# Output product of a second MoE layer: high and low weight halves in one 512-column operand, tokens in blocks of 128

## Chip, cores and metric

One core of a Trainium2 chip runs the whole program. The metric is the device time of one execution in microseconds, lower is better; three timed runs of the kernel before gave 1485.56, 1487.03 and 1487.63 us (median 1487.03).

## What is computed

An attention block between 512 tokens and 32 state rows for 8 batches and 8 heads, then two MoE layers without routing on its 4352 rows of 512 values:

```python
x = concat([xread, sread])                  # attention, 8 x (512 + 32) rows
h = np.maximum(x @ w_in, 0.0)               # 512 -> 2048
x = h * h @ w_out                           # 2048 -> 512
xn = x / rms * rms_g
g = xn @ w_gate                             # 512 -> 1536
silu = g * (1.0 / (1.0 + np.exp(-g)))
return silu * (xn @ w_val) @ w_out          # 1536 -> 512
```

## The kernel before

**Numbers as pairs.** Every operand of a product is split into a high and a low part in a reduced 32-bit float form (`split`, L121: a copy on ScalarE and a subtraction on VectorE). A product is three matmuls into the same bank of PSUM: high by high, high by low, low by high (`mm3`, L125).

**Stages.** Attention and the first MoE run batch by batch until about 735 us. Then come the gate and value products of the second MoE (`moe2_in`, L720): four groups s of two batches, each with 12 steps fc over the hidden width; both tokens of a pair and both weights are combined by a Strassen-like scheme of seven products (`PRODUCTS`, L567) in place of eight, with sums and differences of the operands made beforehand and seven products added into results by `recombine` (L591). In the last group the 256 state rows go along (`moe2_in_sb`, L739). `h_sums` (L762) makes seven operands of the hidden values of a pair of batches, and `h_store` (L775) puts them into DRAM (`hq_dr`).

**The output product before.** First the 256 state rows, with no Strassen scheme: `moe2_out_sb` (L884) makes 12 x 2 x 3 matmuls of 512 columns from tiles `hs`, which hold four steps each and are split by `split_hs` (L879). Then eight blocks blk of 256 tokens of two batches: `load_hb` (L829) reads for each of six weight parts m a tile `hb` (four operands) and a tile `hc` (three) in pieces of 256 floats, `split_hb` (L838) splits them, and `moe2_out` (L847) runs for m, then for the seven products k, then for two halves c of 128 tokens, three matmuls of 256 columns (L859). The token values are the stationary operand, so every matmul has a weight load of 128 columns before it. All seven products of a block accumulate over m in seven PSUM banks; on the last m `recombine` takes each into the tiles `ox` and `oy`, and the store of a batch's rows stands right behind its last addition (L877).

**Weights.** `w2_sums` (L792) makes the differences of the output weights during the first MoE, `w2_split` (L805) makes two high and two low tiles of each part m and stores them in DRAM, and `load_w2` (L813) brings the 24 tiles of 512 KB back for the output stage, where they stay.

**What sets the order.** The order is written out by hand: `put(position, step)` collects events, which are sorted by position and issued in that order on every engine's own queue. A unit of position is a step fc in the gate and value stage (n2 is its end), and one of the six parts m after it. Offsets stand in the table T. All DMAs go through one queue, that of SP, in this order, and each waits there for its data and for a free slot: all tiles come out of one pool of 54 slots of 4 KB per partition. PSUM has eight banks, taken in turn (`any_bank`, L576).

Of the kernel before, what the change touches and what calls it, by code (L numbers as in the profile page):

```python
# [16 lines left out]
P = 128  # L17
# [30 lines left out]
    wq0=-6.06, wq=-1.9, wq_gap=0.27,  # L48
    xl0=-7.97, xsum0=-6.06, xsp0=-3.95, xsp_gap0=0.62, xl=-8.77, xl_gap=0.03, xsum=-4.63, xsp=-3.3, xsp_gap=0.44,
    xsum_gap=0.18, tail=0.3, hsum=0.3, hst=1.47, sbl=-1.3, sbs=-1.03, hs=-1.05, hbl=-3.88, hbs0=-1.5, hbs1=-1.37,  # L50
    w2l=-6.87, w2l_gap=1.18, w2l_i=1.24,
# [6 lines left out]
def attention_moe_kernel(  # L58
# [31 lines left out]
    SB = B  # L90
# [606 lines left out]
    def split_xb(s, name):  # L697
        if (s, name) not in xb:
            return
        t = xb.pop((s, name))  # L700
        if s == SB:
            n = ntok[SB]
            hi = u([P, 2, 512], F32R, "hi")
            nc.scalar.copy(hi[:, :, :n], f(t)[:, :, :n])
            lo = u([P, 2, 512], F32R, "lo")
            nc.vector.tensor_tensor(lo[:, :, :n], f(t)[:, :, :n], f(hi)[:, :, :n], op=ALU.subtract)
        else:
            hi = hi_of(t)
            lo = lo_of(t, hi)
        xq[s, name] = (hi, lo)  # L710
# [28 lines left out]
    def moe2_in_sb(fc):  # L739
        cols = slice((fc % 2) * P, (fc % 2 + 1) * P)  # L740
# [14 lines left out]
        q, r = divmod(fc, 4)  # L755
        if r == 0:
            hs[q] = u([P, 4, 256], F32, "hs")
        t = u([P, 2, 512], F32, "rg")
        nc.scalar.activation(t[:, 0, :n], g, AF.Silu)
        nc.vector.tensor_tensor(hs[q][:, r, :], t[:, 0, :n], v, op=ALU.mult)  # L760
# [14 lines left out]
    def h_store(s, m):  # L775
# [9 lines left out]
        (m, i): dram.tile([P, 2, 512], F32, tag=f"w2_{m}_{i}", name=f"w2_dr{m}_{i}")  # L785
        for m in range(NF2 // 2)
        for i in range(4)
# [4 lines left out]
    def w2_sums(m):  # L792
# [10 lines left out]
        w2s[m] = (w, t.rearrange("p (a q) m -> p a (q m)", a=2))  # L803

    def w2_split(m, i):  # L805
        after(("w2s", m, i))
        t = w2s[m][i]
        hi = hi_of(t)
        lo = lo_of(t, hi)
        nc.sync.dma_start(w2_dr[m, 2 * i], f(hi))  # L810
        nc.sync.dma_start(w2_dr[m, 2 * i + 1], f(lo))

    def load_w2(m, i):  # L813
        after(("ldw2", m, i), ("w2s", m, i // 2))
        w2q[m, i] = u([P, 2, 512], F32R, "w2")
        nc.sync.dma_start(f(w2q[m, i]), w2_dr[m, i])  # L816

    B_AT = dict(b11=(0, 0), b21=(0, 2), b22=(0, 3), t1=(2, 0), t2=(2, 1), t3=(2, 2), t4=(2, 3))

    def w2_part(m, name):  # L820
        i, q = B_AT[name]
        return tuple(
            w2q[m, i + j].rearrange("p a (q m) -> p (a q) m", q=2)[:, q, :] for j in range(2)
        )


    hb = {}

    def load_hb(blk, m):  # L829
        s, ob = divmod(blk, 2)  # L830
        cols = slice(256 * ob, 256 * ob + 256)
        after(("ldhb", blk, m), ("hst", s, m))
        t = [u([P, 4, 256], F32, "hb"), u([P, 4, 256], F32, "hc")]
        nc.sync.dma_start(t[0], hq_dr[s, m][:, :4, cols])
        nc.sync.dma_start(t[1][:, :3, :], hq_dr[s, m][:, 4:, cols])
        hb[blk, m] = t

    def split_hb(blk, m, i):  # L838
        t = hb[blk, m][i]
        n = 4 - i  # L840
        hi, lo = u([P, 4, 256], F32R, "hh"), u([P, 4, 256], F32R, "hl")
        split(t[:, :n, :], hi[:, :n, :], lo[:, :n, :])
        hb[blk, m][i] = (hi, lo)

    acc2 = {}

    def moe2_out(blk, m, k):  # L847
        a, b = PRODUCTS[k]
        last = m == NF2 // 2 - 1
        if m == 0:  # L850
            acc2[blk, k] = any_bank("o2")
        ps = acc2[blk, k]
        i, q = divmod(A_ROW.index(a), 4)
        hi, lo = (t[:, q, :] for t in hb[blk, m][i])
        w_hi, w_lo = w2_part(m, b)
        for c in range(2):
            o = ps[:, 256 * c : 256 * c + 256]
            cols = slice(c * P, (c + 1) * P)
            mm = lambda l, r, start, stop: nc.tensor.matmul(  # L859
                o, l, r, start=start, stop=stop, skip_group_check=True  # L860
            )
            mm(hi[:, cols], w_hi, m == 0 and c == 0, False)
            mm(hi[:, cols], w_lo, False, False)
            mm(lo[:, cols], w_hi, False, last)
        if not last:
            return
# [3 lines left out]
        pv = ps.rearrange("p (c d) -> p c d", c=2)  # L870
        recombine(k, pv, (ox[:, :, :256], ox[:, :, 256:]), (oy[:, :, :256], oy[:, :, 256:]))
        s, ob = divmod(blk, 2)
        for i, done in ((0, 5), (1, 6)):
            if k == done:
                b = 2 * s + i
                rows = out[b * NT : b * NT + S, :].rearrange("(p c) m -> p c m", c=4)
                nc.sync.dma_start(rows[:, 2 * ob : 2 * ob + 2, :], acc2[blk][i])  # L877

    def split_hs(q):  # L879
        hi, lo = u([P, 4, 256], F32R, "hh"), u([P, 4, 256], F32R, "hl")  # L880
        split(hs[q], hi, lo)
        hs[q] = (hi, lo)

    def moe2_out_sb(fc):  # L884
        if fc == 0:
            acc2[SB, 0], acc2[SB, 1] = any_bank("o2"), any_bank("o2")
        q, r = divmod(fc, 4)
        hi, lo = hs[q]
        w_hi, w_lo = w2q[fc // 2, 0][:, fc % 2, :], w2q[fc // 2, 1][:, fc % 2, :]
        for c in range(2):  # L890
            cols = slice(c * P, (c + 1) * P)
            mm3(acc2[SB, c], hi[:, r, cols], lo[:, r, cols], w_hi, w_lo, fc == 0, fc == NF2 - 1)
# [290 lines left out]
```

## Time and profile before

| | us |
|---|---|
| median of three runs | 1487.03 |
| lowest, highest | 1485.56, 1487.63 |
| the profiled execution, its own time | 1484.66 |
| its span, first to last instruction | 1482.6 |

The profile is one execution. The span leaves out 2.1 us at its edges; the profiled execution lies 0.9 us under the lowest timed run. A row of a group by line gives the engine, the operation, output <- inputs with their shapes and count, then the busy time, the mean duration of one and the idle time before it. The duration of a matmul is modelled and longer than the distance between two starts; the distance is read in a timeline. PE is TensorE, PEld its weight loads, DVE is VectorE, ACT is ScalarE, SPq is the DMA queue.

### The profile page before, as it was taken

The numbers are of one execution on the slowest core, as the hardware profiler recorded it, in microseconds if no ns is written. First come the engines' busy times: TensorE is split into PE (matmuls) and PEld (weight loads), VectorE is DVE, ScalarE is ACT, GpSimd is POOL, SyncE is SP. The second block draws the span as 40 slices with busy tenths as digits, with TensorE's granted clock in tenths as the row PEclk, the third lists the DMA queues.
The fourth block names the chain that finished last, engine by engine and source line by source line (L and its number), as shares of the span: only waits on it lengthen the run. The fifth ranks groups of instructions, "written<-read, shape, count | busy, mean of one in ns | idle before, by whom it ended". The sixth has DMA issues, their size and how long they took to land. (4 is left out here: it accounts for less than half of the span.)

```text
span 1482.6 us, 20652 instructions
## 1 busy us (share of the span) xinstructions
PE 1447.2 (98%) x7706; PEld 1248.6 (84%) x7706; DVE 1125.2 (76%) x1654; ACT 783.0 (53%) x1186; POOL 0.7 (0%) x6
## 2 busy tenths in 40 slices
PE   4899999999999999999999999999999999999998
PEld 2688888888888888889987888888888888999998
DVE  7997878999998999874778878978965664565554
ACT  5988768888888888874522211312311123434331
POOL 0000000000000000000000000000000000000000
PEclk7999999999999999999999999999999999999999
DMA  8886443464555555452957897797786869567753
GB/s 321 291 282 226 149 163 121 163 235 166 226 176 219 178 220 180 170 208 72 355 213 279 324 347 282 284 354 279 264 315 221 292 238 339 182 218 242 241 188 107
DMA packets 138420, 345.82 MB, mean 233 GB/s; under 512 B 12112, under 2 KB 56144, under 8 KB 138320
## 3 DMA queue, kind: packets, MB, share of 16 engines
q1 hardware_dynamic: 138320, 344.51, 64.6%
q8 instruction: 60, 0.98, 0.3%
q14 instruction: 40, 0.33, 0.1%
HBM read 229.12 MB, written 115.34 MB: 232 GB/s over the span
## 5 line engine op out<-in xcount | busy, mean ns | idle before, releaser
L126 PE MATMUL p<-hi,wq 128*128 128x512 f32 x672 | 261.7, 389 | 2.0 <-DVE hx L594 2.0
L127 PE MATMUL p<-lo,wq 128*128 128x512 f32 x672 | 261.6, 389 | 0.0
L128 PE MATMUL p<-hi,wq 128*128 128x512 f32 x672 | 261.4, 389 | 0.0
L859 PE MATMUL o<-w,hh 128*128 128x256 f32 x1344 | 242.1, 283 | 0.8 <-ACT hh L122 0.8
L734 ACT ACTIVATE hx<-hx 128x1024 f32<-128x1024 f32 x48 | 50.9, 1061 | 332.9 <-DVE hx L594 332.9
L126 PE MATMUL o<-hl,wh 128*128 128x512 f32 (+1 forms) x576 | 218.8, 380 | 1.1 <-DVE x L518 0.8
L128 PE MATMUL o<-hl,wl 128*128 128x512 f32 (+1 forms) x576 | 217.6, 378 | 0.0
L127 PE MATMUL o<-hl,wh 128*128 128x512 f32 (+1 forms) x576 | 217.5, 378 | 0.0
L859 PEld LDWEIGHTS o<-w,hh 128*128 128x128 f32 x1344 | 209.6, 192 | 1.3 <-ACT hh L122 1.3
L859 PE MATMUL o<-w,hl 128*128 128x256 f32 x672 | 190.4, 283 | 0.8 <-DVE hl L123 0.8
L594 DVE TENSOR_TENSOR hx<-hx,p 128x512 f32<-128x512 f32 x192 | 128.9, 683 | 52.6 <-PE p L128 49.6
L126 PEld LDWEIGHTS p<-hi,wq 128*128 128x128 f32 x672 | 126.2, 188 | 28.2 <-DVE hx L594 2.4
L128 PEld LDWEIGHTS p<-hi,wq 128*128 128x128 f32 x672 | 126.2, 188 | 26.4
L127 PEld LDWEIGHTS p<-lo,wq 128*128 128x128 f32 x672 | 126.2, 188 | 25.5
L490 DVE TENSOR_TENSOR hl<-rg,hl 128x512 fp32r<-128x512 f32 (+1 forms) x144 | 94.6, 657 | 54.3 <-ACT hl L489 53.4
L859 PEld LDWEIGHTS o<-w,hl 128*128 128x128 f32 x672 | 129.0, 192 | 1.1 <-DVE hl L123 1.0
L126 PEld LDWEIGHTS o<-hl,wh 128*128 128x128 f32 x576 | 108.4, 188 | 22.8 <-DVE x L518 2.8
L128 PEld LDWEIGHTS o<-hl,wl 128*128 128x128 f32 x576 | 108.4, 188 | 20.3
L127 PEld LDWEIGHTS o<-hl,wh 128*128 128x128 f32 x576 | 108.4, 188 | 19.8
L126 PE MATMUL h<-at,ph 128*128 128x512 f32 x256 | 102.1, 399 | 5.0 <-ACT pst L260 5.0
L123 DVE TENSOR_TENSOR hl<-hb,hh 128x1024 fp32r<-128x1024 f32 x48 | 58.7, 1222 | 57.1 <-ACT hh L122 57.1
L122 ACT CAST hh<-hb 128x1024 fp32r<-128x1024 f32 x48 | 50.4, 1050 | 95.9 <-DMA hb<-hq_dr 94.6
(169 smaller groups left out, 2592.9 us busy)
## 6 DMA issues: line engine op xcount, KB each, us to landing
wq<-wq_dr SPq DMA_DIRECT2D x168, 512.0 KB, 7.2
hq_dr<-hy SPq DMA_DIRECT2D x48, 512.0 KB, 3.6
hb<-hq_dr SPq DMA_DIRECT2D x48, 512.0 KB, 8.5
hc<-hq_dr SPq DMA_DIRECT2D x48, 384.0 KB, 8.7
raw<-in_moe_w_out_dram SPq DMA_DIRECT2D x30, 512.0 KB, 6.6
p_dr<-pst SPq DMA_DIRECT2D x56, 256.0 KB, 5.5
praw<-p_dr SPq DMA_DIRECT2D x28, 512.0 KB, 5.3
wq_dr<-hi SPq DMA_DIRECT2D x24, 512.0 KB, 2.9
```

What stands on the lines that cost most here:

```text
L122: nc.scalar.copy(hi, src)
L123: nc.vector.tensor_tensor(lo, src, f(hi), op=ALU.subtract)
L126: nc.tensor.matmul(ps, lh, rh, start=start, stop=False)
L127: nc.tensor.matmul(ps, lh, rl, start=False, stop=False)
L128: nc.tensor.matmul(ps, ll, rh, start=False, stop=stop)
L490: nc.vector.tensor_tensor(t[:, 1, :n], rg[:, 1, :n], f(t[:, 0, :n]), op=ALU.subtract)
L594: add = lambda o, i, p: nc.vector.tensor_tensor(o, i, p, op=ALU.add)
L734: nc.scalar.activation(x, x, AF.Silu)
L859: mm = lambda l, r, start, stop: nc.tensor.matmul(o, l, r, start=start, stop=stop, skip_group_check=True)
```

## The change

The output product takes 128 tokens at a time: 16 blocks of tokens, and before them one block with the state rows, which now goes through the seven products too (`hs_sums` makes its four further operands on the chip). The weights' high and low halves lie side by side, so one matmul of 512 columns multiplies the tokens' high part by both, and a second one of 256 columns multiplies the low part by the high half; `recombine` works on 512 columns with both halves, and one more addition folds the two halves before the store. A block runs in two halves of three parts m, with k outside m. Loads of the token tiles are one DMA of 448 KB with pieces of 128 floats for a block and part, placed earlier by a lead that grows over the first blocks; splits likewise; stores are placed 1.5 units behind. Weight tiles: 21 in place of 24. Offsets in the gate and value stage change as well. Below, unchanged lines and blank ones are thinned out, and the removal of `split_hs` and `moe2_out_sb`, which stood where the dots are, is left out.

```diff
@@ -45,10 +45,11 @@
-    wq0=-6.06, wq=-1.9, wq_gap=0.27,
-    xl0=-7.97, xsum0=-6.06, xsp0=-3.95, xsp_gap0=0.62, xl=-8.77, xl_gap=0.03, xsum=-4.63, xsp=-3.3, xsp_gap=0.44,
-    xsum_gap=0.18, tail=0.3, hsum=0.3, hst=1.47, sbl=-1.3, sbs=-1.03, hs=-1.05, hbl=-3.88, hbs0=-1.5, hbs1=-1.37,
-    w2l=-6.87, w2l_gap=1.18, w2l_i=1.24,
+    wq0=-6.06, wq=-3, wq_gap=0.33,
+    xl0=-7.97, xsum0=-6.09, xsp0=-3.95, xsp_gap0=0.62, xl=-8.78, xl_gap=0.03, xsum=-6.57, xsp=-4.14, xsp_gap=0.62,
+    xsum_gap=0.11, tail=0.3, hsum=0.43, hst=1.88, sbl=-2.06, sbs=-0.91, hss=0.2,
+    hbl=-8, hbl_gap=1.0, hbl_e=1.0, hbs=-4.8, hbs_gap=1.0, hbs_e=0.4, w2a=-4, ost=1.5, w2b=-1.6, 
+    w2l_gap=.6, w2l_i=.12,
 )
@@ -752,12 +752,23 @@
         product(g, "a12", "b21", False)
         product(v, "s1", "b11", True)
         product(v, "a22", "t4", False)
-        q, r = divmod(fc, 4)
+        m, r = divmod(fc, 2)
         if r == 0:
-            hs[q] = u([P, 4, 256], F32, "hs")
+            hs[m] = u([P, 7, P], F32, "hs")
         t = u([P, 2, 512], F32, "rg")
         nc.scalar.activation(t[:, 0, :n], g, AF.Silu)
-        nc.vector.tensor_tensor(hs[q][:, r, :], t[:, 0, :n], v, op=ALU.mult)
+        both = hs[m][:, 2 * r : 2 * r + 2, :]
+        halves = lambda ap: ap.rearrange("p (c t) -> p c t", c=2)
+        nc.vector.tensor_tensor(both, halves(t[:, 0, :n]), halves(v), op=ALU.mult)
+    def hs_sums(m):
+        after(("hs", m), ("sb", 2 * m), ("sb", 2 * m + 1))
+        a = [hs[m][:, i, :] for i in range(7)]
+        sub = lambda o, i, j: nc.vector.tensor_tensor(a[o], a[i], a[j], op=ALU.subtract)
+        nc.vector.tensor_tensor(a[4], a[1], a[3], op=ALU.add)
+        sub(5, 4, 0)
+        sub(1, 0, 1)
+        sub(6, 2, 5)
     def h_sums(s, m):
@@ -782,9 +793,9 @@
     w2_dr = {
-        (m, i): dram.tile([P, 2, 512], F32, tag=f"w2_{m}_{i}", name=f"w2_dr{m}_{i}")
+        (m, i): dram.tile([P, 2, 2, 256], F32, tag=f"w2_{m}_{i}", name=f"w2_dr{m}_{i}")
         for m in range(NF2 // 2)
-        for i in range(4)
+        for i in range(3 + (m + 1) % 2)
     }
     w2s = {}
     w2q = {}
@@ -800,105 +811,96 @@
         sub(t[:, 2, :], b22, b12)
         sub(t[:, 1, :], b22, t[:, 0, :])
         sub(t[:, 3, :], b21, t[:, 1, :])
-        w2s[m] = (w, t.rearrange("p (a q) m -> p a (q m)", a=2))
+        w2s[m] = (b[:, :, :256], t[:, :2, :], t[:, 2:, :], b[:, 1:, 256:])
     def w2_split(m, i):
         after(("w2s", m, i))
-        t = w2s[m][i]
-        hi = hi_of(t)
-        lo = lo_of(t, hi)
-        nc.sync.dma_start(w2_dr[m, 2 * i], f(hi))
-        nc.sync.dma_start(w2_dr[m, 2 * i + 1], f(lo))
+        src = w2s[m][i]
+        n = src.shape[1]
+        t = u([P, 2, 2, 256], F32R, "w2s")
+        split(src, t[:, :n, 0, :], t[:, :n, 1, :])
+        if i == 3:
+            nc.sync.dma_start(w2_dr[m - m % 2, 3][:, m % 2], f(t)[:, 0])
+            return
+        nc.sync.dma_start(w2_dr[m, i], f(t))
     def load_w2(m, i):
-        after(("ldw2", m, i), ("w2s", m, i // 2))
-        w2q[m, i] = u([P, 2, 512], F32R, "w2")
+        if i == 3 and m % 2:
+            return
+        after(("ldw2", m, i), ("w2s", m, i), ("w2s", m + (i == 3), i))
+        w2q[m, i] = u([P, 2, 2, 256], F32R, "w2")
         nc.sync.dma_start(f(w2q[m, i]), w2_dr[m, i])
-    B_AT = dict(b11=(0, 0), b21=(0, 2), b22=(0, 3), t1=(2, 0), t2=(2, 1), t3=(2, 2), t4=(2, 3))
+    B_AT = dict(b11=(0, 0), b21=(0, 1), t1=(1, 0), t2=(1, 1), t3=(2, 0), t4=(2, 1), b22=(3, 0))
     def w2_part(m, name):
         i, q = B_AT[name]
-        return tuple(
-            w2q[m, i + j].rearrange("p a (q m) -> p (a q) m", q=2)[:, q, :] for j in range(2)
-        )
+        if i == 3:
+            m, q = m - m % 2, m % 2
+        return w2q[m, i].rearrange("p q j d -> p q (j d)")[:, q, :]
     hb = {}
+    hq = {}
     def load_hb(blk, m):
-        s, ob = divmod(blk, 2)
-        cols = slice(256 * ob, 256 * ob + 256)
+        s, c = divmod(blk, 4)
         after(("ldhb", blk, m), ("hst", s, m))
-        t = [u([P, 4, 256], F32, "hb"), u([P, 4, 256], F32, "hc")]
-        nc.sync.dma_start(t[0], hq_dr[s, m][:, :4, cols])
-        nc.sync.dma_start(t[1][:, :3, :], hq_dr[s, m][:, 4:, cols])
-        hb[blk, m] = t
-    def split_hb(blk, m, i):
-        t = hb[blk, m][i]
-        n = 4 - i
-        hi, lo = u([P, 4, 256], F32R, "hh"), u([P, 4, 256], F32R, "hl")
-        split(t[:, :n, :], hi[:, :n, :], lo[:, :n, :])
-        hb[blk, m][i] = (hi, lo)
+        hb[blk, m] = u([P, 7, P], F32, "hb")
+        nc.sync.dma_start(hb[blk, m], hq_dr[s, m][:, :, c * P : (c + 1) * P])
+    def split_hb(blk, m):
+        hi, lo = u([P, 7, P], F32R, "hh"), u([P, 7, P], F32R, "hl")
+        if blk == 2 * B:
+            after(("hsplit", m), ("hs", m))
+            split(hs.pop(m), hi, lo)
+        else:
+            split(hb.pop((blk, m)), hi, lo)
+        hq[blk, m] = (hi, lo)
     acc2 = {}
-    def moe2_out(blk, m, k):
+    HALF = NF2 // 4
+    def moe2_out(blk, half, k):
         a, b = PRODUCTS[k]
-        last = m == NF2 // 2 - 1
-        if m == 0:
+        if half == 0:
             acc2[blk, k] = any_bank("o2")
         ps = acc2[blk, k]
-        i, q = divmod(A_ROW.index(a), 4)
-        hi, lo = (t[:, q, :] for t in hb[blk, m][i])
-        w_hi, w_lo = w2_part(m, b)
-        for c in range(2):
-            o = ps[:, 256 * c : 256 * c + 256]
-            cols = slice(c * P, (c + 1) * P)
-            mm = lambda l, r, start, stop: nc.tensor.matmul(
+        i = A_ROW.index(a)
+        for m in range(half * HALF, (half + 1) * HALF):
+            hi, lo = hq[blk, m]
+            w = w2_part(m, b)
+            mm = lambda o, l, r, start, stop: nc.tensor.matmul(
                 o, l, r, start=start, stop=stop, skip_group_check=True
             )
-            mm(hi[:, cols], w_hi, m == 0 and c == 0, False)
-            mm(hi[:, cols], w_lo, False, False)
-            mm(lo[:, cols], w_hi, False, last)
-        if not last:
+            mm(ps, hi[:, i, :], w, m == 0, False)
+            mm(ps[:, :256], lo[:, i, :], w[:, :256], False, m == 2 * HALF - 1)
+        if half == 0:
             return
         if k == 0:
             acc2[blk] = [u([P, 2, 512], F32, "ox"), u([P, 2, 512], F32, "oy")]
         ox, oy = acc2[blk]
-        pv = ps.rearrange("p (c d) -> p c d", c=2)
-        recombine(k, pv, (ox[:, :, :256], ox[:, :, 256:]), (oy[:, :, :256], oy[:, :, 256:]))
-        s, ob = divmod(blk, 2)
+        recombine(k, ps, (ox[:, 0, :], ox[:, 1, :]), (oy[:, 0, :], oy[:, 1, :]))
         for i, done in ((0, 5), (1, 6)):
             if k == done:
-                b = 2 * s + i
-                rows = out[b * NT : b * NT + S, :].rearrange("(p c) m -> p c m", c=4)
-                nc.sync.dma_start(rows[:, 2 * ob : 2 * ob + 2, :], acc2[blk][i])
...
+                t = acc2[blk][i]
+                o = t[:, :, :256]
+                nc.vector.tensor_tensor(o, o, t[:, :, 256:], op=ALU.add)
+    def store_out(blk, i):
+        o = acc2[blk][i][:, :, :256]
+        halves = lambda rows: rows.rearrange("p (a d) -> p a d", a=2)
+        if blk == 2 * B:
+            for q in range(4):
+                r0 = (4 * i + q) * NT + S
+                nc.sync.dma_start(halves(out[r0 : r0 + NS, :]), o[32 * q : 32 * q + 32])
             return
+        s, c = divmod(blk, 4)
+        r0 = (2 * s + i) * NT
+        rows = out[r0 : r0 + S, :].rearrange("(p c) m -> p c m", c=4)
+        nc.sync.dma_start(halves(rows[:, c, :]), o)
     sources = {"win": w_in, "wout": w_out, "wg": w_gate, "wv": w_val, "w2": w_out2}
@@ -1000,21 +1002,25 @@
     for name in ("b11", "b21", "t4"):
         put(e + T["sbs"] + 0.3, split_xb, SB, name)
     nout = NF2 // 2
-    for fc in range(NF2):
-        put(n2 + fc / 2, moe2_out_sb, fc)
-    for q in range(NF2 // 4):
-        put(n2 + 2 * q + T["hs"], split_hs, q)
-    for blk in range(B):
-        e = n2 + (blk + 1) * nout
+    for m in range(nout):
+        put(n2 - NF2 + 2 * m + 2 + T["hss"], hs_sums, m)
+    for q, blk in enumerate([2 * B] + list(range(2 * B))):
+        e = n2 + q * nout
+        early = min(max(q - 1, 0), 3)
         for m in range(nout):
+            h, r = divmod(m, HALF)
+            if blk < 2 * B:
+                put(e + HALF * h + T["hbl"] - T["hbl_e"] * early + T["hbl_gap"] * r, load_hb, blk, m)
+            put(e + HALF * h + T["hbs"] - T["hbs_e"] * early + T["hbs_gap"] * r, split_hb, blk, m)
+        for h in range(2):
             for k in range(7):
-                put(e + m + k / 7, moe2_out, blk, m, k)
-            put(e + m + T["hbl"], load_hb, blk, m)
-            put(e + m + T["hbs0"], split_hb, blk, m, 0)
-            put(e + m + T["hbs1"], split_hb, blk, m, 1)
+                put(e + HALF * (h + k / 7), moe2_out, blk, h, k)
+        for i in range(2):
+            put(e + HALF * (1 + (5 + i) / 7) + (T["ost"] if q < 2 * B else 0.0), store_out, blk, i)
     for m in range(nout):
         for i in range(4):
-            put(n2 + T["w2l"] + T["w2l_gap"] * m + T["w2l_i"] * i, load_w2, m, i)
+            h, r = divmod(m, HALF)
+            put(n2 + T["w2b" if h else "w2a"] + T["w2l_gap"] * r + T["w2l_i"] * i, load_w2, m, i)
     halves = ("xt", "st", "toka", "tokb", "at", "ex", "r2", "e2t", "xn", "sr")
@@ -1059,7 +1065,7 @@
             put(pos + T["dsp"] + T["dsp_gap"] * m, wq_split, c2, m)
         convert(pos + T["e0"], ("w2", c2), split=False)
         put(pos + T["e_sum"], w2_sums, c2)
-        for i in range(2):
+        for i in range(4):
             put(pos + T["e_sp"] + T["e_spgap"] * i, w2_split, c2, i)
     for fq in range(NFQ1):
         for k2 in range(2):
```

## Rows read from the trace of the kernel before

**Rows 1.** Page, busy us of each engine over the span
```profile
PE 1447.2 (98%) x7706; PEld 1248.6 (84%) x7706; DVE 1125.2 (76%) x1654; ACT 783.0 (53%) x1186; POOL 0.7 (0%) x6
```

**Rows 2.** Chain of waits that ended last, pieces: start us, us, what
```profile
1224.56 7.99 DMA hb<-hq_dr
...
1234.99 241.38 PE o L859 x2008
```

**Rows 3.** Groups by line, second output product: xcount | busy us, mean ns
```profile
L859 PE MATMUL o<-w,hh 128*128 128x256 f32 x1344 | 242.1, 283 | 0.8 <-ACT hh L122 0.8
L859 PE MATMUL o<-w,hl 128*128 128x256 f32 x672 | 190.4, 283 | 0.8 <-DVE hl L123 0.8
L126 PE MATMUL o<-w,hh 128*128 128x512 f32 x24 | 9.3, 390 | 0.0
```

**Rows 4.** Timeline of TensorE, 512 columns: start us, us, what
```profile
999.83 0.39 PE L128 MATMUL p<-hi,wq 128*128 128x512 f32 x1
...
1003.91 0.39 PE L128 MATMUL p<-hi,wq 128*128 128x512 f32 x1
```

**Rows 5.** Busy us of each engine by stretch, clock, DMA
```profile
core 0: us, PE busy (x) PEld busy (x) DVE busy (x) ACT busy (x) POOL busy (x), PEclk, DMA share, GB/s
965.00:1080.00 115.00, 115.00 (x520) 95.74 (x519) 96.67 (x134) 26.50 (x34) 0.00 (x0) 1.00 0.81 303
1080.00:1216.00 136.00, 136.00 (x723) 117.79 (x722) 83.99 (x123) 25.00 (x37) 0.00 (x0) 1.00 0.70 253
1216.00:1235.00 19.00, 17.41 (x80) 14.03 (x78) 6.47 (x9) 3.79 (x5) 0.00 (x0) 1.00 1.04 397
1265.00:1295.00 30.00, 30.00 (x253) 30.00 (x252) 16.51 (x20) 11.04 (x14) 0.00 (x0) 1.00 0.69 220
```

**Rows 6.** Timeline of TensorE where the token output product starts
```profile
1232.51 0.39 PE L128 MATMUL o<-w,hl 128*128 128x512 f32 x1
1233.73 0.51 PE L859 MATMUL o<-w,hh 128*128 128x256 f32 x2 [0.84 <-ACT hh L122]
1234.99 0.39 PE L859 MATMUL o<-w,hl 128*128 128x256 f32 x1 [0.76 <-DVE hl L123]
```

**Rows 7.** Timeline of the DMA queue SP: start us, us, issues
```profile
1224.56 0.46 SPq L834 DMA_DIRECT2D hb<-hq_dr  x1
...
1254.43 1.27 SPq L835 DMA_DIRECT2D hc<-hq_dr  x1
1268.00 0.36 SPq L877 DMA_DIRECT2D out_dram<-ox  x1
```

**Rows 8.** Waits of SP: us in total, times, longest us
```profile
SPq L877 <- DVE ox L594: 123.0, 8, 23.7
...
SPq L816 <- PE p L128: 23.7, 4, 13.8
```

**Rows 9.** Timeline of TensorE at a stop in the gate product
```profile
805.11 0.39 PE L128 MATMUL p<-hi,wq 128*128 128x512 f32 x1
807.49 0.47 PE L126 MATMUL p<-hi,wq 128*128 128x512 f32 x1 [1.99 <-DVE hx L594]
```

**Rows 10.** Groups by line, VectorE and ScalarE: xcount | busy us, mean ns
```profile
L123 DVE TENSOR_TENSOR hl<-hb,hh 128x1024 fp32r<-128x1024 f32 x48 | 58.7, 1222 | 57.1 <-ACT hh L122 57.1
L123 DVE TENSOR_TENSOR hl<-hc,hh 128x768 fp32r<-128x768 f32 x48 | 45.7, 952 | 1.4 <-ACT hh L122 1.4
L122 ACT CAST hh<-hb 128x1024 fp32r<-128x1024 f32 x48 | 50.4, 1050 | 95.9 <-DMA hb<-hq_dr 94.6 <-DMA hc<-hq_dr 0.7 <-PE o L859 0.7
L594 DVE TENSOR_TENSOR ox<-ox,o 128x512 f32<-128x512 f32 x32 | 21.8, 684 | 61.7 <-PE o L859 60.8
```

**Rows 11.** DMA issues: KB each, median us to landing
```profile
hb<-hq_dr SPq DMA_DIRECT2D x48, 512.0 KB, 8.5
...
out_dram<-oy SPq DMA_DIRECT2D x8, 512.0 KB, 4.0
```

**Rows 12.** Timeline of the end
```profile
1478.27 0.35 SPq L877 DMA_DIRECT2D out_dram<-oy  x1
```

More of the change, by code (lines that the diff above doesn't have):

```diff
@@ L701, in split_xb @@
         if s == SB:
[L702 to L706, printed above, removed]
+            both = u([P, 2, 2, ntok[SB]], F32R, "hl")
+            hi, lo = both[:, 0], both[:, 1]
+            split(f(t)[:, :, : ntok[SB]], hi, lo)
         else:
@@ L739, in moe2_in_sb @@
     def moe2_in_sb(fc):
+        after(("sb", fc))
         cols = slice((fc % 2) * P, (fc % 2 + 1) * P)
@@ L869, in moe2_out @@
         ox, oy = acc2[blk]
-        pv = ps.rearrange("p (c d) -> p c d", c=2)
-        recombine(k, pv, (ox[:, :, :256], ox[:, :, 256:]), (oy[:, :, :256], oy[:, :, 256:]))
-        s, ob = divmod(blk, 2)
+        recombine(k, ps, (ox[:, 0, :], ox[:, 1, :]), (oy[:, 0, :], oy[:, 1, :]))
         for i, done in ((0, 5), (1, 6)):
             if k == done:
-                b = 2 * s + i
-                rows = out[b * NT : b * NT + S, :].rearrange("(p c) m -> p c m", c=4)
-                nc.sync.dma_start(rows[:, 2 * ob : 2 * ob + 2, :], acc2[blk][i])
[L879 to L892, printed above, removed]
-        if fc < NF2 - 1:
-            return
-        t = u([P, 2, 512], F32, "os")
-        nc.scalar.copy(t[:, 0, :], acc2[SB, 0])
-        nc.vector.tensor_copy(t[:, 1, :], acc2[SB, 1])
-        for c in range(2):
-            for q in range(4):
-                r0 = (4 * c + q) * NT + S
-                nc.sync.dma_start(out[r0 : r0 + NS, :], t[32 * q : 32 * q + 32, c, :])
+                t = acc2[blk][i]
[8 more added lines that the diff above has]
+                nc.sync.dma_start(halves(out[r0 : r0 + NS, :]), o[32 * q : 32 * q + 32])
+            return
+        s, c = divmod(blk, 4)
+        r0 = (2 * s + i) * NT
+        rows = out[r0 : r0 + S, :].rearrange("(p c) m -> p c m", c=4)
+        nc.sync.dma_start(halves(rows[:, c, :]), o)
     sources = {"win": w_in, "wout": w_out, "wg": w_gate, "wv": w_val, "w2": w_out2}
```

## Prediction

> **What bounds the kernel now.** I read the page first: TensorE is busy for 98% of the span [rows 1], and in the stages that the change touches the granted clock is 1.00, so it runs at its upper level of 2.4 GHz [rows 5]. At 98% only two things can shorten the kernel: less work on TensorE, or fewer of its stops. The chain of waits says the same of the stage that is changed: it ends in one unbroken piece of 2008 matmuls of line 859 in 241.38 us, that is 120.2 ns each [rows 2], and before it stands a load of a token tile. The groups by line give the counts: 1344 and 672 matmuls of 256 columns, and 24 (three times, once for each line of `mm3`) of 512 columns for the state rows [rows 3]. Their mean durations (283 and 390 ns) are modelled and overlap; what counts is the distance of starts.
>
> **The price of a matmul.** In the 512-column timeline 18 distances take 1003.91 - 999.83 = 4.08 us, so 226.7 ns each [rows 4]. With 256 columns it is 120.2 ns [rows 2]. The difference is 106.5 ns for 256 columns, which is 2.4 columns per ns; so each matmul costs its columns plus a fixed 13.7 ns, with a new weight load before each in both cases. The change keeps the number of columns and takes away a third of the matmuls, so the fixed part is what it can win.
>
> The Trainium skill, TensorE: Matmul & The Clock Gate, in the section "Wait — 56ns, not 53.3ns?", gives a fixed part of about 2.5 ns for warm back-to-back matmuls. This case's rows show 13.7 ns at both sizes; by the page, as an estimate, 672 matmuls less would give 1.7 us and the state rows 1.9 us, 3.6 us where terms 1 and 2 below have 10.9.
>
> **Term 1, token blocks: -9.2 us.** Before, 128 tokens, one product and one part m cost 3 x 120.2 = 360.6 ns. After, one matmul of 512 and one of 256 columns: 226.7 + 120.2 = 346.9 ns. There are 16 x 6 x 7 = 672 such groups: 672 x 13.7 = 9.2 us. Lower and upper end are close, since both prices are measured at full clock; the one open point is whether the weights of a 512-column matmul load in the shadow of a 256-column one, and in the present stage every load does just that, with a new one each 120 ns.
>
> **Term 2, state rows: -1.7 us.** Before 72 matmuls of 512 columns [rows 3, 4]: 16.3 us. After, seven products: 42 pairs x 346.9 = 14.6 us. The price for it, additions on VectorE and larger splits, lies beside TensorE in a stage where VectorE has room (last group, below).
>
> **Term 3, the start of the output product: -0.6 us.** Now TensorE stops twice here, 0.84 + 0.76 us by the waits [rows 6], because the first token tile is issued at 1224.56 and lands 8 us later [rows 2, 7]; it stands behind weight loads that waited 23.7 us in all for slots that TensorE frees [rows 8]. After, the first token tiles are put in front of the second half of the weight loads and have 14.6 us of state rows as cover, so the 1.6 us should go. What is late next are the weights: the state rows used to need 12 of the tiles over 16 us, now they need 11 in their first 7.3 us and the other 10 by then. If the ten (5.2 MB) came only after n2, at the 350 GB/s that 512 KB loads reach in a burst, they would take 15 us and stop TensorE for 7.7 us. They are placed 1.6 units, some 20 us, ahead of n2, and that is nearest to the present small stop; I leave 1 us of new stop. Ends: -1.6 and +6.
>
> **Term 4, offsets in the gate and value product: -1.0 us.** TensorE has one stop there, 1.99 us, behind VectorE [rows 9]; the sums of the next group's operands pile up with the fold work. They move 1.9 units, about 18 us, earlier, and the weight loads 1.1 units. VectorE is 84% busy in this stage [rows 5], so the pile may shrink or arise elsewhere. Ends: -2.0 and +1.5; I take half the gain.
>
> **Term 5, the end: -0.3 us.** The last store is issued at 1478.27 [rows 12] and a store of 512 KB lands after 4.0 us [rows 11]. After, the fold of both halves adds one more addition of 512 columns, 0.68 us [rows 10], and the last stores are 256 KB each, some 0.7 to 1.5 us less to move for the two. Ends: -1 and +0.5.
>
> **What costs nothing, and its cover.** VectorE, for a block of 14.57 us (42 x 346.9 ns): six splits of 896 elements, between 952 ns for 768 and 1222 ns for 1024 [rows 10], so 1087 ns each, 6.5 us; seven folds and two additions of 0.684 us, 6.2 us; 12.7 us, 87%, against 55% now (16.51 of 30 us [rows 5]). The folds, which wait for TensorE, come in the second half of a block only, so VectorE falls behind there by some 3 us and makes it up in the first half of the next; a bank is needed again about three units, 7 us, after its fold was due. If VectorE fell more than that behind, TensorE would wait for banks. ScalarE has six copies of about 0.94 us (1.05 us for 1024 elements [rows 10]) and one more: no bound. The DMA queue: as many token loads as now (96), with 448 KB each. The stores now stand on SP right behind the fold they wait for, 123.0 us of waiting in eight pieces [rows 8], and the next block's loads queue behind: 1254.43 to 1268.00 nothing is issued [rows 7], and then twelve come in a burst. TensorE doesn't wait for that even now, so moving stores by 1.5 units gives nothing by itself, but it spreads the loads, which the next point needs. The four splits of a weight part in place of two handle fewer elements (1792 for 2048) and lie in the first MoE beside TensorE.
>
> **Pieces of 512 bytes.** Token loads now come in pieces of 1 KB: share 0.69 at 220 GB/s is 51 ns for a piece on one of 16 DMA engines; in the stage with pieces of mostly 4 KB, share 0.81 at 303 GB/s is 175 ns [rows 5]. The line through both is 10 ns plus 41 ns per KB, so 31 ns for 512 bytes. No row has a 512-byte piece: it lies between half of 51 and 51. By 31 ns a block's 5376 pieces take 10.4 us on 16 engines, its stores 1.6: 12 of 14.57 us, hidden. By 51 ns they take 17.3 + 1.6 = 18.9 us and the loads set the pace. I take 31, on the line between the two rows; up to 38 ns the loads stay within a block's time and cost nothing.
>
> **Sum.** -9.2 - 1.7 - 0.6 - 1.0 - 0.3 = -12.8 us. The profiled execution took 1484.66 us (its span is 1482.6), so 1471.9 there. The timed runs have their median 2.4 us above it, at 1487.03; I put the same difference on top: **1474.2 us**.
>
> **Rivals.**
> 1. **Weights late for the state rows.** The stop of term 3 at its full size: -9.2 - 1.7 + 6 - 1.0 - 0.3 = -6.2 us gives 1480.8. For it: the weight loads wait for slots today, and the stretch around 1216 to 1235 has a full DMA share (1.04 [rows 5]). Against: three fewer weight tiles are moved, and their place in the queue is 20 us ahead. Chance 0.11.
> 2. **Slower: the 512-byte pieces cost as much as 1 KB.** A block takes 18.9 instead of 14.57 us, 16 x 4.3 = 69 us, less some 12 us of lead (five units) and the 12.8 us won: 1531 us. It decides from 43 ns a piece upward, where a block takes 16.1 us and 16 x 1.5 us equal lead and gain together. For it: no row has such a piece, and VectorE's folds stand behind the splits that wait for loads. Against: the line through the rows. Chance 0.05.
> 3. **The fixed part isn't saved.** If the 13.7 ns went with the columns, at 226.7 / 512 = 0.443 ns each, term 1 would be nothing and term 2 would be its 4608 columns less, 2.0 us: -3.9 in all, 1483.1. Against: that price makes a matmul of 256 columns 113 ns, and 120.2 were measured. Chance 0.04. By the 2.5 ns of the Trainium skill (TensorE: Matmul & The Clock Gate, the section named above) it would be -5.5 us, 1481.5; that is the same rival with another price.
> 4. **The change doesn't do what it says:** the weights of the wide matmul don't load beside the narrow one and the pair takes 360 ns or more, so that only the smaller terms remain: 1484 to 1490. Against it stands the same load every 120 ns now. Chance 0.03.
>
> **How the numbers follow.** The forecast has the remaining 0.77. Its own range is 1470.5 to 1478: terms 3 to 5 at their lower ends give 1.9 us less than the sum plus a microsecond or two of scatter, as the three runs have, and upward the stops of terms 3 and 4 cost 4 us between them. To hold eight in ten with rival 1 in part, the range is 1470.5 to 1480.5. A measurement can tell about 0.2%, 3 us: faster than 1484.1 are the forecast (0.77), rival 1 (0.11) and half of rival 3 (0.02): 0.90; within 3 us the other half of it and rival 4: 0.05; slower, rival 2: 0.05.
>
> **What would show it.** Right: 1344 + 84 matmuls in the output product, starts 227 and 120 ns apart in turn, a stage of about 248 us in place of 260; VectorE near 85% there, DMA share near 0.8 without bursts. Wrong: TensorE idle behind the split of a token tile at each block (rival 2), one stop of several us inside the state rows' block behind weight tiles (rival 1), or pairs longer than 347 ns (rivals 3, 4).

## Result and profile after

Four runs of the changed kernel gave 1468.71 to 1470.40 us, median 1469.19; four of the kernel before in the same setting 1485.56 to 1487.63, median 1486.34. The ratio is 0.9885, 95% interval [0.9868, 0.9902]. The direction was right, but the time lies 1.3 us under the range of 1470.5 to 1480.5. The profiled execution took 1470.4 us, the slowest of the four; its span is 1468.6 us, 14.0 us less than before. In the experiments below one execution of the kernel before, beside the second series of the changed one, ran at a granted clock of 0.65 and took 2069.82 us; it is left out of every median.

The page of the changed kernel, engines over the span (answers to [rows 1]), then its groups of the output product ([rows 3]):

```profile
PE 1435.6 (98%) x7046; PEld 1211.2 (82%) x7046; DVE 1191.3 (81%) x1789; ACT 785.2 (53%) x1209; POOL 0.7 (0%) x6
...
L875 PE MATMUL o<-w,hh 128*128 128x512 f32 x714 | 248.1, 392 | 0.0
...
L875 PE MATMUL o<-w,hl 128*128 128x256 f32 x714 | 200.3, 281 | 0.6 <-DVE hl L124 0.6
```

660 matmuls fewer, as the change says: 714 wide and 714 narrow in place of 2088. A stretch of the changed kernel (answers to [rows 5]; start:end, us, busy us of each engine, granted clock, DMA share, GB/s):

```profile
1295.00:1325.00 30.00, 30.00 (x175) 26.47 (x174) 24.41 (x32) 11.48 (x14) 0.00 (x0) 1.00 0.83 229
```

The groups on VectorE and ScalarE (answers to [rows 10]):

```profile
L124 DVE TENSOR_TENSOR hl<-hb,hh 128x896 fp32r<-128x896 f32 x96 | 102.0, 1086 | 40.8 <-ACT hh L123 40.4
...
L123 ACT CAST hh<-hb 128x896 fp32r<-128x896 f32 x96 | 85.8, 942 | 34.5 <-DMA hb<-hq_dr 23.5
```

The waits of SP from 1180 us on (answers to [rows 8]; us in total, times, longest us), where 123.0 us in eight pieces behind VectorE became 83.2 in fourteen:

```profile
SPq L903 <- DVE ox L890: 83.2, 14, 12.8
SPq L852 <- PE o L875: 44.7, 29, 3.4
```

The page's DMA issues of the token loads (answers to [rows 11]; KB each, median us to landing), 448 KB in pieces of 512 bytes, landing sooner than the 512 KB before:

```profile
hb<-hq_dr SPq DMA_DIRECT2D x96, 448.0 KB, 6.7
```

And the end (answers to [rows 12]), where one more addition stands ahead of the last store:

```profile
1464.66 0.69 DVE L890 TENSOR_TENSOR oy<-oy 128x512 f32<-128x512 f32 x1
```

VectorE went from 55% to 81% in the output stage (87% forecast), the DMA share from 0.69 to 0.83 (12 of 14.57 us forecast), and TensorE, busy for 30.00 of the 30 us, still doesn't wait there. Taken apart by starts of matmuls, the two profiled executions differ so:

| stretch | before | after | difference | forecast |
|---|---|---|---|---|
| to the first gate product | 719.2 | 719.7 | +0.5 | 0 |
| gate and value stage | 497.2 | 494.9 | -2.3 | -1.0 |
| output stage, first to last matmul | 260.4 | 248.7 | -11.7 | -11.5 |
| after the last matmul | 5.9 | 5.3 | -0.6 | -0.3 |

Below, lost time is what the distances between the starts of matmuls have above the flat price (one ns for 2.4 columns, and 13.3 ns). The +0.5 hides three things: the first matmul starts 0.5 us later (7.20 for 6.71 us); the first 60 us lose 1.3 us more (32.1 for 30.8; over all traces below the first gate product begins between 717.8 and 720.8 us); and from 60 us on the first MoE loses 1.3 us less (6.9 for 8.2).

### The profile page after: what moved, and what is told of

The parts are those of the page before. It is cut to its first block, busy times and chain, and to the rows that moved or that the text cites. A ratio compares the mean times of both kernels' runs of the same rounds, so it can differ in the third digit from the quotient of the medians.

```text
span 1468.6 us, 19494 instructions
## 1 busy us (share of the span) xinstructions
PE 1435.6 (98%) x7046; PEld 1211.2 (82%) x7046; DVE 1191.3 (81%) x1789; ACT 785.2 (53%) x1209; POOL 0.7 (0%) x6
## 4 chain that ended last, share of the span: by engine, by line
PE 78%; DVE 10%; ACT 6%; DMA 2%; issue 1%; SPq 0%; DVEq 0%; ACTq 0%
PE o L875 15%; PE p L127 10%; PE p L129 10%; PE p L128 10%; PE o L127 5%; PE o L129 5%; PE o L128 5%; PE h L127 3%; PE h L128 3%; PE h L129 3%; DVE hl L491 1%; DMA hb<-hq_dr 1%; DVE pl L124 1%; ACT rg L488 1%; ACT rg L487 1%
## 5 line engine op out<-in xcount | busy, mean ns | idle before, releaser
L875 PE MATMUL o<-w,hh 128*128 128x512 f32 x714 | 248.1, 392 | 0.0
L875 PE MATMUL o<-w,hl 128*128 128x256 f32 x714 | 200.3, 281 | 0.6 <-DVE hl L124 0.6
L875 PEld LDWEIGHTS o<-w,hh 128*128 128x128 f32 x714 | 133.6, 187 | 29.4
L875 PEld LDWEIGHTS o<-w,hl 128*128 128x128 f32 x714 | 135.3, 190 | 0.9 <-DVE hl L124 0.9
L124 DVE TENSOR_TENSOR hl<-hb,hh 128x896 fp32r<-128x896 f32 x96 | 102.0, 1086 | 40.8 <-ACT hh L123 40.4
L123 ACT CAST hh<-hb 128x896 fp32r<-128x896 f32 x96 | 85.8, 942 | 34.5 <-DMA hb<-hq_dr 23.5
```

The lines of the kernel that those rows point to most:

```text
L123: nc.scalar.copy(hi, src)
L124: nc.vector.tensor_tensor(lo, src, f(hi), op=ALU.subtract)
L875: mm = lambda o, l, r, start, stop: nc.tensor.matmul(o, l, r, start=start, stop=stop, skip_group_check=True)
```

## Experiments

Eighteen more series ran, two of them of the changed kernel unaltered. Medians stand against the kernel before on the same chip. A pair is a wide matmul (512 columns) and a narrow one (256); its pace is read from the starts of wide matmuls. The parts are undone or done alone; none leaves out a part of the product, and one adds the low by low products.

### The changed kernel twice more

No edit.

> The changed kernel, unaltered, once more. Theory A (the changed offsets were worth more than the 1.0 us of term 4, and the rest of the miss is scatter of single executions, above all in the first 60 us): 1469 to 1471 us, 15 to 17 us under the kernel before in the same rounds; the trace again has no stop between 800 and 850 us. Theory B (the output product itself won more than 10.9 us): the same time, but the product's stage, from its first matmul to the last, is shorter than 248 us.

> The changed kernel, unaltered, for the third time, as the measure for the two kernels beside it. Theory C2 (an execution keeps one of two rhythms of wide and narrow matmuls until TensorE is stopped): the times fall into two groups some 4 to 5 us apart, 1469 to 1471 and 1473 to 1475 us; the traced execution shows 346.7 ns a pair where it stopped before and 353.3 ns where it didn't.

The second time the runs were 1469.21, 1469.70, 1471.86, 1473.81 and 1474.37 (median 1471.86, ratio 0.9914 [0.9899, 0.9930]), the third time 1468.47 to 1474.51 (median 1469.39, ratio 0.9900 [0.9885, 0.9915]). The medians of the three series lie 17.2, 13.8 and 15.8 us under those of the kernel before on the same chip. The second is above theory A's 1469 to 1471 us and inside the forecast range, and its traced output stage took 252.2 us, against theory B's less than 248. So one kernel has times 5 us apart, and where the median of four or five runs falls changes with the series. What differs between three traced executions shows in their chains of waits (start us, us, what), first that of the result above:

```profile
1238.58 224.00 PE o L875 x1291
```

The second time:

```profile
1214.82 251.24 PE o L875 x1422
```

The third time:

```profile
1236.87 228.30 PE o L875 x1291
```

Per pair (two matmuls) that is 347.0, 353.4 and 353.7 ns. The same instructions run at two rhythms. In the timeline of TensorE the short one, from the first profile, returns every 346.7 ns:

```profile
1300.17 0.39 PE L875 MATMUL o<-w,hh 128*128 128x512 f32 x1
...
1303.64 0.39 PE L875 MATMUL o<-w,hh 128*128 128x512 f32 x1
```

Ten pairs in 3.47 us. The long rhythm, of the second time, has a cycle of three pairs, 1060 ns:

```profile
1300.16 0.40 PE L875 MATMUL o<-w,hh 128*128 128x512 f32 x1
...
1303.70 0.40 PE L875 MATMUL o<-w,hh 128*128 128x512 f32 x1
```

Ten pairs in 3.54 us. 714 x 6.7 ns = 4.8 us is about the distance of the two groups of times. That the untraced executions divide by the rhythm is likely but not shown: one execution of each series has a trace, and starts alone vary by up to 3 us. Every traced execution with wide and narrow in turn enters the stage in the long rhythm. The first profile left it at a stop of TensorE for the split of a token tile; the second one never stopped and stayed long (251.24 us in one piece), and the third, against its expectation, stopped at the same place and went on long. The stop of the first profile, in the timeline:

```profile
1238.58 0.39 PE L875 MATMUL o<-w,hl 128*128 128x256 f32 x1 [0.58 <-DVE hl L124]
```

### One size instead of two

```diff
 e_three256
-            mm(ps, hi[:, i, :], w, m == 0, False)
+            mm(ps[:, :256], hi[:, i, :], w[:, :256], m == 0, False)
+            mm(ps[:, 256:], hi[:, i, :], w[:, 256:], False, False)
 e_hi_lo_hi: the same three, the low part's between the two of the high part
 e_all_wide
-            mm(ps[:, :256], lo[:, i, :], w[:, :256], False, m == 2 * HALF - 1)
+            mm(ps, lo[:, i, :], w, False, m == 2 * HALF - 1)
```

> The changed kernel with the 512-column matmul cut into two of 256 columns, so three matmuls and three weight loads for a group again. Fixed part of 13.7 ns: 714 x 13.7 = 9.8 us more than the changed kernel, some 1479 us, the stage 258.5 in place of 248.7 us. If the product won more than its sum (theory B): 12 us more or above. If the fixed part were 2.5 ns: 1.8 us more.

> The changed kernel with the 512-column matmul cut into two of 256, as in the run with three of 256 columns, but in the order high, low, high, so that no matmul has the stationary tile of the one before it. If it is the mix of sizes that makes the rhythm: 120.0 ns each as in the other order, a stage of 257 us. If it is that every weight load brings a new tile: more than 120 ns, about 123, a stage of 261 us or more.

> The changed kernel with the low part multiplied by both halves of the weights too, so all matmuls of the output stage have 512 columns and each has a new stationary tile; it adds the low by low products to the sums. If the mix of sizes makes the rhythm: 226.7 ns each, 1428 x 226.7 = 323.7 us for the stage. If new tiles do it: about 234.5 ns, as wide after wide in the grouped run, 334.9 us.

Chain of waits of the first, three of 256 columns:

```profile
1213.14 255.97 PE o L875 x2133
```

The same in the order high, low, high:

```profile
1214.03 255.97 PE o L875 x2133
```

All of 512 columns:

```profile
1213.62 322.36 PE o L875 x1422
```

120.0, 120.0 and 226.7 ns each, with hardly a deviation in the stage. So new stationary tiles (the tile that a weight load brings) cost nothing; with one size the price is fixed, and the two rhythms were seen only where sizes are mixed. The first one's time is 1476.90 (ratio 0.9952 [0.9939, 0.9965]): 5.0 us over the changed kernel's median on the same chip, 8.2 us over the first profile's stage. The forecast 9.8 us holds against the short rhythm only (714 x 13.3 = 9.5 us by the flat prices; the first profile spent its first 24 us in the long one and 0.7 us in the stop). The other two ran once each, 1477.75 and 1543.81 us.

### Wide after wide

```diff
+        for m in range(half * HALF, (half + 1) * HALF):
+            mm(ps, hq[blk, m][0][:, i, :], w2_part(m, b), m == 0, False)
         for m in range(half * HALF, (half + 1) * HALF):
+            w = w2_part(m, b)
+            mm(ps[:, :256], hq[blk, m][1][:, i, :], w[:, :256], False, m == 2 * HALF - 1)
```

> The changed kernel with the order inside a product turned: the three 512-column matmuls of the three parts first, then the three of 256 columns. Theory C (wide and narrow in turn have two steady rhythms, 346.7 and 353.3 ns a pair, and each execution falls into one of them): with wide after wide and narrow after narrow only the fixed prices are left, the stage is 247.5 to 248.5 us in every execution and the times of all runs lie within 2 us of each other, near 1469. Theory D (the 3.5 us between two executions of the changed kernel come from the tiles' addresses or the loads, not from the turns): the spread and the mean stay as in the changed kernel repeated, 1469 to 1474.

Four runs within 0.9 us, 1471.27 to 1472.21, ratio 0.9904 [0.9890, 0.9917]: one rhythm, as theory C has it, but not the short one. The stage took 250.2 us, 350 ns a pair; wide after wide took 234.5 ns here, against 226.7 where all are wide. Six matmuls took 1050 ns, where theory C's fixed prices make 1040, so its second half fell; the excess stands at wide after wide, and why is not shown.

### Which of the two comes first, and a shift

```diff
 e_narrow_first: the two calls exchanged, start and stop with them
 e_nudge (at each block), e_nudge_q2 (k == 0 and blk == 1), e_nudge_sb (k == 1 and blk == 2 * B)
+            if m == 0 and k == 0:
+                mm(ps[:, :P], hi[:, i, :], w[:, :P], True, False)
```

> The changed kernel with the 256-column matmul ahead of the 512-column one in every pair; the work is the same. Theory C2, if the rhythm is set by which of the two comes first after the matmuls before it: one group of times instead of two, 1469 to 1471 us if it enters the short rhythm (the rhythm was short in the traces after TensorE had stopped ahead of a narrow one). Theory E (the rhythm is set by the addresses or by chance): two groups as in the unaltered kernel.

> The changed kernel with one more matmul of 128 columns ahead of each of the 17 blocks, into a bank that the next matmul starts anew; it computes nothing that is kept. Its own price is 17 x 67 = 1.1 us. Theory C2: it shifts the turns, so the rhythm can change at a block's start and a trace shows 346.7 and 353.3 ns in different blocks, or the short one everywhere: 1470 to 1473 us. Theory E: two groups of times, each 1.1 us later.

> The changed kernel with a single extra matmul of 128 columns ahead of the second product of the state rows; it computes nothing that is kept. Every trace so far enters the stage at 353.4 ns a pair, and in the run with 17 nudges each nudge turned the rhythm. Theory C2: from the nudge on 346.7 ns a pair, until TensorE stops near 1236 us, after which it can be either; where there is no stop it stays short to the end: most times near 1469 us. Theory E (the rhythm doesn't depend on such a shift): 353.4 ns goes on.

> The changed kernel with the single extra matmul ahead of the second token block, after the place of the stop. Theory C2: it turns whatever rhythm is there, so an execution that was long becomes short from there and the reverse: still two groups of times, 4 us apart, with a trace that changes near 1244 us. Theory E: no change there.

Narrow first: 1468.31 to 1475.62 us in two groups, long in the traced execution; the order is not it. A nudge is an extra matmul of 128 columns whose result is not kept. With 17 nudges the blocks after the stop went 356.0, 349.4, 356.0, 349.4 ns a pair in turn (2.7 ns of it the nudge, 113 ns for one in place of the 67 expected): there each nudge turned the rhythm, median 1473.34, all five runs within 1.2 us. Of the single nudges, the one in the state rows turned nothing: the rhythm stayed long up to the stop at 1237 us and was short behind that stop (trace 1469.90 us, median 1471.46). The one at the second block did turn it: the rhythm was short behind the stop, from 1238 us on, and long from the nudge to the end (median 1473.19), which is the change near 1244 us that theory C2 expected of the trace. TensorE's timeline has ten pairs in 3.47 us before the nudge and in 3.52 us behind it (the nudge is shown merged with the wide matmul after it):

```profile
1240.04 0.39 PE L875 MATMUL o<-w,hh 128*128 128x512 f32 x1
...
1243.51 0.39 PE L875 MATMUL o<-w,hh 128*128 128x512 f32 x1
...
1243.85 0.51 PE L875 MATMUL o<-w,hh 128*128 128x128 f32 x2
...
1244.33 0.40 PE L875 MATMUL o<-w,hh 128*128 128x512 f32 x1
...
1247.85 0.40 PE L875 MATMUL o<-w,hh 128*128 128x512 f32 x1
```

So theory C2 holds in part: a shift can turn the rhythm, but doesn't do so everywhere. Which nudges did has an order to it. The long cycle is three pairs with distances of 241 + 120, 236 + 113 and 233 + 117 ns. Over the traces with nudges, all nine that met the short rhythm made it long; of ten that met the long one, the eight that came behind its third pair made it short, and the two that came behind its second pair (in the state rows, here and in the run with both edits below) left it long.

### The stop near 1236 us

```diff
-                put(e + HALF * h + T["hbl"] - T["hbl_e"] * early + T["hbl_gap"] * r, load_hb, blk, m)
+                put(e + HALF * h + T["hbl"] - T["hbl_e"] * (early or 1.0) + T["hbl_gap"] * r, load_hb, blk, m)
 e_lead_nudge: with e_nudge_sb's matmul besides
```

> The changed kernel with the first token block's loads one unit earlier. If the stop near 1236 us comes from the place of these loads in the queue: no stop in the trace, so the rhythm stays as it entered, 353.3 ns to the end, and all times lie in the upper group, 1473 to 1475 us. If the weight loads ahead of them set it: the stop stays.

> Both: loads of the first token block one unit earlier, and the one extra matmul ahead of the second product of the state rows. Theory C2: no stop and the short rhythm from the second product to the end, stage of 248 us, all times in one group near 1468.5 us, below the changed kernel's median. Theory E: as with the earlier loads alone.

With the earlier loads no stop, and 251.24 us in one piece of 1422 matmuls: long throughout. All four runs lie at 1471.56 to 1472.98, the tight group that was expected, though a microsecond lower. With the nudge the same, 1472.34 to 1473.64: the hope for the short rhythm in every execution fell. It is the odd result of this study that with a stop of 0.75 us taken away the median, 1472.72, is higher than that of all 14 unaltered runs on other chips, 1469.56 (against the kernel before on its own chip the ratio is 0.9904, within the 0.9885 to 0.9914 of the three series).

### Offsets of the gate and value stage

```diff
 e_old_offsets (in the changed kernel); e_before_new_offsets is the reverse in the kernel before, without sbl, sbs
-    wq=-3, wq_gap=0.33, xsum=-6.57, xsp=-4.14, xsp_gap=0.62, xsum_gap=0.11, hsum=0.43, hst=1.88, sbl=-2.06, sbs=-0.91
+    wq=-1.9, wq_gap=0.27, xsum=-4.63, xsp=-3.3, xsp_gap=0.44, xsum_gap=0.18, hsum=0.3, hst=1.47, sbl=-1.3, sbs=-1.03
```

(`xl` and `xsum0` follow by 0.01 and 0.03.)

> The changed kernel with the offsets of the gate and value stage as before (loads, sums and splits of the token operands, weight loads, sums and stores of the hidden values, state-row loads). Theory A: the stop of 2.2 us behind VectorE is back near 805 us, 2.3 us more than the changed kernel in the trace, 1471 to 1473 us. Theory B: under 0.7 us more and no such stop.

> The kernel before with the new offsets of the gate and value stage and nothing else of the change. Theory A: 2.3 us less in the trace, the stop near 805 us gone, 1483 to 1485 us. Theory B: the same as before within 0.7 us.

In the kernel before, the new offsets alone gave 1482.84 against 1485.70, ratio 0.9984 [0.9976, 0.9993], and the gate stage took 494.9 us, as after the change: the whole stop of [rows 9] is gone. The first of the two stops of [rows 6] shrank as well: the output stage took 259.7 in place of 260.4 us. Put back into the changed kernel the old ones cost more than the stop of before: 1479.58 (ratio 0.9965 [0.9952, 0.9978]), a gate stage of 499.4 us with two stops in TensorE's timeline, the first of them now behind a weight load rather than VectorE, the second new:

```profile
806.77 0.47 PE L127 MATMUL p<-hi,wq 128*128 128x512 f32 x1 [1.53 <-DMA wq<-wq_dr]
...
1200.22 0.47 PE L127 MATMUL p<-hi,wq 128*128 128x512 f32 x1 [2.43 <-DVE hx L595]
```

Theory A had 2.3 us here and the trace shows 4.5. The second stop lies in the last group, where VectorE now has the state rows' sums to make; that these cause it is not shown. The traced execution was the fastest of the six, and their median lies 7.7 us above the changed kernel's, so what the slower ones lost besides is open.

### Splits of the output weights

```diff
 e_split_places (changed kernel)
-            put(pos + T["e_sp"] + T["e_spgap"] * i, w2_split, c2, i)
+            put(pos + T["e_sp"] + T["e_spgap"] * (i // 2), w2_split, c2, i)
 e_before_half_splits (kernel before)
-        hi = hi_of(t)
-        lo = lo_of(t, hi)
+        hi, lo = u([P, 2, 512], F32R, "hi"), u([P, 2, 512], F32R, "lo")
+        for j in range(2):
+            split(f(t)[:, j, :], hi[:, j, :], lo[:, j, :])
```

> The changed kernel with the third and fourth split of each output-weight part at the places of the first two, rather than 0.33 and 0.66 units later. If the places took away the short stops of the first MoE: the lost time between 60 us and the first gate product goes from 6.9 back to 8 us. If not, it stays near 7.

> The kernel before, with each split of an output-weight tile made as two copies and two subtractions of 512 columns in place of one of 1024 each; nothing else. If the smaller pieces took away TensorE's short stops at the ends of the batches in the first MoE (8.2 us of lost time between 60 us and the first gate product before, 6.9 after): 1 us less in that stretch of the trace. If the places of the splits did it: no difference in that stretch.

With the places put together the lost time between 60 us and the first gate product is back at 8.2 us (6.9 in the changed kernel), and the waits of TensorE in 60 to 720 us show again what the changed kernel no longer has (us in total, times, longest):

```profile
PE o L127 <- DVE x L519: 1.2, 3, 0.6
```

Its times, 1470.50 to 1474.16, can't show 1.2 us beside the rhythm. Smaller pieces alone in the kernel before did nothing good: ratio 0.9997 [0.9988, 1.0006], lost time 9.4 us. The sixteen traces with the spread places lose 6.8 to 7.5 us there, the four without them 8.1 to 9.4. The places are the cause.

### Places of stores and loads

```diff
 e_store_at_fold
-ost=1.5
+ost=0.0
 e_no_growth
-hbl_e=1.0, hbs_e=0.4
+hbl_e=0.0, hbs_e=0.0
```

> The changed kernel with the stores right behind the last addition in place of 1.5 units later. If the stores' place only spreads the loads, as the prediction has it: TensorE's time in the output stage the same, within 1 us, and more of SP's time waiting for VectorE. If loads behind a waiting store arrive late: stops of TensorE behind token tiles at each block, 16 times up to 2 us, 1475 us or above.

> The changed kernel with the lead of loads and splits kept as in the first block (no growth). Pieces of 512 bytes cost 30 ns each, 12 of 14.6 us of a block, so loads have little room to catch up: by the prediction's count a lead of five units before the split falls to two and a token tile that lands after 6.7 us is late by 1 to 2 us now and then, 1470 to 1485 us. If the loads have ample room: the same time as the changed kernel.

Stores at the fold: 1470.23 to 1476.09, median 1474.65, ratio 0.9915 [0.9900, 0.9929]; the trace has small stops between 1236 and 1253 us, 1.9 us in all, and none after; it is the fastest of the five, so what the slower ones lost is not shown. No growth: 1469.21 to 1474.32, one stop of 1.45 us in the first token block, then none. In the traces neither place is worth more than these stops, and the loads have room once the start is past: 512-byte pieces took 30.4 ns on average (31 forecast).

## Why the prediction was right or wrong

**Two steps failed: half the gain of term 4, and the splits put at nothing.** Each left out 1.3 us, and both lie outside the new product.

**Term 4, -1.0 us: mis-sized.** "I take half the gain" failed. The stop went whole, -2.3 us in the trace. Half was taken because the pile on VectorE might arise elsewhere; it didn't, neither in the changed kernel nor in the kernel before with the offsets alone. The runs of the latter give 1485.70 - 1482.84 = 2.9 us, which fits: in its trace the offsets also took 0.7 us from the stops of term 3.

**"The four splits ... lie in the first MoE beside TensorE": wrong.** Spread over 0.66 units more, they took away 1.3 us of TensorE's short stops behind VectorE. I had not read the waits of that stretch.

**Terms 1 and 2, -10.9 us: right in size, wrong as a constant.** The starts of the kernel before lie 226.7 and 120.0 ns apart (the 120.2 of [rows 2] has the ends of its piece in it, so the fixed part is 13.3 ns and not 13.7), and the short rhythm's pair is their sum, 346.7 ns: 2016 x 120.0 + 72 x 226.7 = 258.2 us before, 714 x 346.7 = 247.5 after, -10.7. As a constant "226.7 + 120.2 = 346.9 ns" fails: the trace of before has no stretch of wide and narrow in turn, and there the pair costs 346.7 or 353.3 ns, as the execution falls. This error makes the kernel slower than forecast and so can't have put the time under the range. Rival 4 named the place (a wide matmul's weights beside a narrow one) but not this size; of its price, 13 ns a pair, half comes in the long rhythm. I gave no range for it.

**Term 3, -0.6 us: also small.** 1.9 us of stops at [rows 6] became 0.7, 0, or 0.7 us in the three traces of the changed kernel. They stand behind a token tile, not behind weights: rival 1 didn't come.

**The 2.4 us on top.** Adding it is the same as taking the gain off the median of three runs. But single executions scatter: before, the profiled one lay 1.7 us under the median of four, and in the changed kernel it was the slowest of four, 1.2 us above theirs. So the two profiled executions differ by 14.3 us and the medians by 17.2.

**The range.** Terms 3 to 5 at their lower ends give 1.0 + 1.0 + 0.7 = 2.7 us less than the sum, not 1.9. With 2.7 the lower bound would be 1469.7, still above the 1469.19.

**Together.** In the short rhythm the traces give -10.7 - 1.2 - 2.3 - 1.3 - 0.6 = -16.1 us; the forecast was -12.8. The medians differ by 1486.34 - 1469.19 = 17.2 us, and the 1.1 us left over is less than single starts scatter. Over all 14 runs of the changed kernel 9 lie below 1470.5 us and 5 within the range, the latter up to 1474.5: that all four runs of the first series fell below is partly luck. The step from within to below is probably the rhythm, as in the traced executions; that the whole lies low is term 4 and the splits.

**Rivals 2 and 3 fell.** Pieces of 512 bytes cost 30.4 ns, on the line of [rows 5]. The fixed part is 13.3 ns by the flat prices. The Trainium skill, TensorE: Matmul & The Clock Gate, section "Wait — 56ns, not 53.3ns?", has about 2.5 ns for back-to-back matmuls, and this case's traces, with a new weight load before each matmul, don't agree with it.

**Term 5** went the right way, -0.6 for -0.3. The covers held: VectorE at 81% and SP's waits of 83.2 us in 14 pieces for the fold cost TensorE nothing in the trace.

## What to carry to other kernels

A price per matmul read where all have one size need not hold where two sizes alternate; measure the mixed sequence itself before summing it. A stop of the bound engine behind a crowded one was worth its whole length here once the work was spread, so read the waits of every stretch whose positions change, also of the "free" ones. A kernel with two groups of times needs more than the four or five runs of one series here, whose medians lay 2.7 us apart, and one profiled execution says nothing of which group is the usual one.

## What the hardware showed unexpectedly

Wide and narrow matmuls in turn run at 346.7 ns or at 353.3 ns a pair with the same instructions, at a granted clock of 1.00, and keep it for hundreds of pairs. One size is exact: 2140 distances of 120 ns out of 2141, and 226.7 ns on average over 1427. Wide after wide takes 234.5 ns when narrow ones stand in the same product. All traced executions with wide and narrow in turn entered in the long rhythm. It became short only after a stop of TensorE (in the first profile, with stores at the fold, with no growth of the lead, and with a single nudge in the state rows or at the second block) or at a nudge behind the third pair of the long cycle; after other stops, such as that of the third series, it stayed long. Every nudge that met the short rhythm turned it long. What inside TensorE sets it stays open, and no version tried has been shown to have the short rhythm in every run.
